# Chunk attention and a SoLU layer: scratch of the squares in the queries' buffers, z's SyncE transfers issued at the turn, sums of w_in's blocks one tile sooner

## The chip, the cores and the metric

One core of a Trainium2 chip. The metric is the device time of one execution in microseconds (us). Its engines here are PE (TensorE, matmuls; PEld is its weight load), DVE (VectorE), ACT (ScalarE), POOL (GpSimd) and SP (SyncE, which only issues transfers). An engine runs its own instructions in the order of the program.

## The reference, cut to what matters

Attention in chunks of 64 positions, then one feed-forward layer with SoLU and a LayerNorm; everything in fp32.

```python
# q, k, v: 8 batches, 8 heads, 576 positions, 64 wide
q_c, k_c, v_c = chunks of 64 positions
s = (q_c @ k_c.T) / 8
p = exp(s - max(s)); p = p / (sum(p) + 1e-9)
x = (p @ v_c), heads side by side          # 4608 tokens x 512
h = x @ w_in                               # 512 -> 1024
e = exp(h - max(h))
solu = h * e / (sum(e) + 1e-9)
ln = (solu - mean) / sqrt(var + 1e-6) * g_ln
out = ln @ w_out                           # 1024 -> 512
```

## The kernel before, in words

The 4608 tokens are 36 tiles of 128. An fp32 product is made on TensorE out of three: each operand is split into a high part (rounded, "top" in the names of the helpers) and the rest ("bottom"), and high x low, high x high and low x high are summed. ACT makes the tops, DVE or POOL the bottoms. A tile passes through these steps: turn of q and k into qT and kT (DVE), scores (PE), softmax (DVE for the row maximum, ACT for the exp, POOL for the division), a turn of the probabilities by 32x32 blocks into a_b (DVE) with four transfers from SBUF to SBUF that put the blocks where they belong (attn_t), values (PE), which gives x with the model's columns on the partitions, the product with w_in (h), exp and SoLU (z), the square for the variance (ACT), a turn of z by 32x32 blocks into z_b (DVE), sixteen transfers z_b to z_t, the split of z_t into z_h and z_l, and the product with w_out into the bank "po" (ffn_out), in three parts called thirds. ACT scales po by r, the inverse of the spread, into o_sb, and SP stores it. Each engine's order is that of the program: the class Order (line 39) keeps it.

Tiles 0 to 4 follow an order written out by hand (START, line 19). Tiles 5 to 9 are single: the loop at line 1192. From tile 10 on the tiles go in pairs (PAIRS, line 97; pair(), line 1089; 13 calls). A pair makes h of two tiles by seven products where eight were needed before (a scheme like Strassen's: the two tiles are the halves of the rows, two halves of d_model, two halves of d_ff; strassen(), line 942). For it w_in's four blocks B11 to B22 need four sums or differences, t1 to t4, and x needs s1 to s4. These are made once, for w_in, by POOL while the single tiles run: t_room (line 880) takes the buffers, t_sum (870) adds blocks into a raw buffer with whole 128x1024 operations, t_top (889, on ACT) and t_bottom (892, on POOL) split that, and t_quarter (896) does sum and split of a quarter on POOL alone, four operations. Where they stand before: t_room and t_sum(B22, B12) at the start of tile 6; t3's top and bottom and t_sum(None, (), B11) after tile 6's variance; t2's top and bottom in tile 7, before solu_b; the last buffers and four quarters of t1 at the start of tile 8; one quarter of t4 after the product of tile 9, three more in pair(10) under `if opening`. The sums of x for pair i+2 are x_sums (line 1050, POOL), x_halves (1058, ACT and POOL) and x_top, x_bottom.

In pair(i) PE runs, in order: a11, s2, s1, s3; three thirds of out1 (tile i-3); s4, a12, a22; the attention of tiles i+2 and i+3 (their values, and scores two tiles on); three thirds of out0 (tile i-2). z_h and z_l of out1 are made at the pair's head, those of out0 beside s4 (z_top, on ACT) and after a22 in program order (z_bottom, on DVE). z_h, z_l and z_b have one buffer, z_t two.

What the change touches:

- variance(i) (line 600) squares z of tiles 0 to 9, spread(i) (line 1033) that of the pairs: ACT writes the squares into a scratch tile "sq", of which only the row sum is used. Both take it from the tag "o_sb" (two buffers), which the scaled output takes too. The queries' tag "qT" (qk_tiles, line 246) has two buffers as well; in pair(i) the order of what spread and turn take is spread(i-1), turn(i+4), turn(i+5), spread(i).
- moves() (line 1070) lists the 16 transfers of z, those with x+y odd on POOL's queue and the others on SP's; pair_moves (1078) returns the list and issue(todo, n) (1084) issues the next n of it. pair(i) makes the list for z of pair i-2 at its head, issues 4 of it after s1 (two on SP, two on POOL), and 12 after attn_turn has turned the probabilities and issued the four moves of attn_t (SP two, and POOL two up to tile 12, later ACT). The two turns of z (pair_turn) are DVE's last work of the pair before.
- The sums of w_in's blocks, as above.

SP also issues the loads of q and k (load_some, up to 9 at two places of a pair), of v, and the stores of the output (store_rest); the loads of a batch are there only in some pairs.

Of the kernel before, what the change touches and what calls it, by code (L numbers as in the profile page):

```python
# [58 lines left out]
def chunk_attention_then_solu_ffn(  # L59
# [13 lines left out]
    DM, FF = H * D, g_ln.shape[0]  # L73
    P = 128
# [784 lines left out]
    TW = {}  # L859
# [10 lines left out]
    def t_sum(of, less, more=()):  # L870

        f = raw_t[0]
        if of is not None:
            pool.tensor_tensor(out=f, in0=f32(of)[0], in1=f32(of)[1], op=ALU.add)
        for x in f32(less):
            pool.tensor_tensor(out=f, in0=f, in1=x, op=ALU.subtract)
        for x in f32(more):
            pool.tensor_tensor(out=f, in0=f, in1=x, op=ALU.add)

    def t_room():  # L880
        def room(dt):
            return work.tile([P, NCH2, HALF], dt, name="t_w", tag="w_a", bufs=5)
        raw_t.append(room(F32))
        TW["t3"] = room(F32R), t_low
        TW["t2"] = room(F32R), room(F32R)
        t1 = room(F32R)
        return lambda: TW.update(t1=(t1, room(F32R)), t4=block(upper, right))
# [145 lines left out]
    def spread(i):  # L1033
        z, esum = st.pop((i, "z"))
        eps = small.tile([P, 1], F32, name="eps")
        act.activation(eps, esum, AF.Square, scale=1e-3, bias=tiny)
        sq = work.tile([P, FF], mybir.dt.bfloat16, name="sq", tag="o_sb")
        ssq = small.tile([P, 1], F32, name="ssq")
        act.activation(sq, z, AF.Square, scale=1.0 / (FF * 32), accum_out=ssq)
        st[i, "v"] = z, ssq, eps  # L1040
# [26 lines left out]
                scores(m + 2)  # L1067
            values(m)

    def moves(zt, of):  # L1070
        for x in range(4):
            for y in range(4):
                yield (pool if (x + y) % 2 else sync).dma_start, (
                    zt[x * 32:(x + 1) * 32, y, of].rearrange("p s a t -> p (s a t)"),
                    turned["b"][y * 32:(y + 1) * 32, x, of].rearrange("p s a t -> p (s a t)"),
                )

    def pair_moves(m, alone=False):
        zt = work.tile([P, 4, 2, NFC, 32], F32, name="z_t")
        for n in (m,) if alone else (m, m + 1):  # L1080
            st[n, "zr"] = zt
        return list(moves(zt, slice(0, 1 if alone else 2)))

    def issue(todo, n):
        for f, args in todo[:n]:
            f(*args)
        del todo[:n]

    def pair(i):
        opening, closing = i == first_pair, i + 2 >= NT  # L1090
        if not banks:
            whole_h.close()
            ps_b = ctx.enter_context(tc.tile_pool(name="ps_b", bufs=1, space=PSUM))
            banks.extend(ps_b.tile([P, HALF], F32, name=n) for n in ("pa", "pb"))
        a, b = banks
        h0, h1 = (work.tile([P, FF], F32, name="z") for _ in range(2))
        HZ[i], HZ[i + 1] = h0, h1
        out1 = queue[0][0]
        softs = pending[:]
        pending.clear()  # L1100
        zmoves = [] if opening else pair_moves(i - 2)

        z_top(out1)
        strassen(i, "a11", a, B11)
        act.copy(h0[:, left], a)
        z_bottom(out1)
        for m in softs[:1]:
            softmax_e(m)
        strassen(i, "s2", b, TW["t2"])
        h_sum(h0[:, right], h0[:, left], b)  # L1110
        x_top(i, "s3")
        x_bottom(i, "s3")
        for m in softs[1:]:
            softmax_e(m)
        strassen(i, "s1", a, TW["t1"])
        issue(zmoves, 4)
        for m in softs:
            whole(softmax_b(m))
        evict()
        strassen(i, "s3", b, TW["t3"])  # L1120
        if not opening:
            spread(i - 1)
        for n in ("s4", "a12", "a22"):
            x_top(i, n)
        h_sum(h1[:, left], h0[:, right], b)
        x_bottom(i, "s4")
        for m in softs:
            attn_turn(m)
        if opening:
            for x in range(1, 4):  # L1130
                t_quarter("t4", B21, TW["t2"], x)
        issue(zmoves, 12)
        least1 = h_out((h1[:, left], h1[:, right]), a, None)
        dve.tensor_tensor(out=h0[:, right], in0=h0[:, right], in1=a, op=ALU.add)
        for p in range(1 if closing else 3):
            product()
        for n in ("a12", "a22"):
            x_bottom(i, n)
        if not opening:
            power(i - 2)  # L1140
            power(i - 1)
        for m in (i + 4, i + 5):
            if m < NT:
                turn(m)
        load_some(9)
        store_rest()

        out0 = queue[0][0]
        waits = (soon.pop(i + 2, []) + soon.pop(i + 3, []))[::-1]
        strassen(i, "s4", a, B22, waits, 6 * NCH2)  # L1150
        if not closing:
            kept.append(out1)
            evict()
            z_top(out0)
        least0 = h_out((h0[:, right], h0[:, right]), a, None)
        strassen(i, "a12", b, B21, waits, 3 * NCH2)
        least0 = h_out((h0[:, left], h0[:, left]), b, least0)
        strassen(i, "a22", a, TW["t4"], waits)
        pair_exp(i, 0, least0)
        least1 = h_out((h1[:, left], h1[:, left]), a, least1)  # L1160
        pair_exp(i, 1, least1)
        if closing:
            return
        z_bottom(out0)
        attention(i)
        for m in (i + 4, i + 5):
            if m < NT:
                load_v(m)
        x_pair(i + 2)
        x_sums(i + 2)  # L1170
        pair_mul(i)
        pair_mul(i + 1)
        for _ in range(3):
            product()
        kept.append(out0)
        pair_mean(i)
        spread(i)
        x_halves(i + 2)
        if i + 4 < NT:
            softmax_a(i + 4)  # L1180
            pending.append(i + 4)
        pair_mean(i + 1)
        pair_turn(i)
        if i + 5 < NT:
            softmax_a(i + 5)
            pending.append(i + 5)
        pair_turn(i + 1)
        load_some(9)
        store_rest()

    first_pair = PAIRS
    for i in range(first, first_pair):
        order.on = i >= ORD
        odd = i % 2 == 1
        turning = i + 1 == first_pair
        if i == first:
            z_turn(i - 1)
            load_batch(next_batch)
            next_batch += 1
        load_v(i + 3)  # L1200
        z_split(queue[0][0], slice(0, NFC))
        if not odd:
            softmax_e(i + 3)
            whole(softmax_b(i + 3))
            attn_turn(i + 3)
            x_high(i + 1)
            if i == first_pair - 4:
                rest_of_room = t_room()
                t_sum(B22, B12)
            if i == first_pair - 2:  # L1210
                rest_of_room()
                for x in range(4):
                    t_quarter("t1", B12, B11, x)
        load_some(LOADS[i][0])
        whole(ffn_in(i))
        if odd:
            for m in (i + 1, i + 2):
                scores(m + 2)
                values(m)
        if turning:  # L1220
            load_v(i + 4)
            for x in range(1):
                t_quarter("t4", B21, TW["t2"], x)
        whole(solu_a(i))
        third()
        if odd:
            softmax_a(i + 3)
            softmax_e(i + 3)
            if turning:
                x_pair(i + 1)  # L1230
                x_sums(i + 1)
            else:
                x_high(i + 1)
        else:
            x_low(i + 1)
        if i == first_pair - 3:
            t_top("t2")
            t_bottom("t2")
        whole(solu_b(i))
        if odd:  # L1240
            if turning:
                x_halves(i + 1)
            else:
                x_low(i + 1)
            whole(softmax_b(i + 3))
            attn_turn(i + 3)
        else:
            for m in (i + 4, i + 5):
                turn(m)
        third()  # L1250
        variance(i)
        if i == first_pair - 4:
            t_top("t3")
            t_bottom("t3")
            t_sum(None, (), B11)
        third()
        load_some(LOADS[i][1])
        z_turn(i)
        store_rest()
        if odd:  # L1260
            softmax_a(i + 4)
            if turning:
                pending.append(i + 4)
# [55 lines left out]
```

## Time and profile before

| | |
|---|---|
| Two timed runs | 527.69 and 529.74 us, median 528.72 |
| The profiled execution's own time | 529.91 us |
| Its span, first to last instruction | 528.1 us |
| Mean granted TensorE clock | 0.976 |
| Busy: PE | 473.2 us, 90% of the span, 4115 matmuls |
| PEld | 364.2 us, 69% |
| DVE | 362.4 us, 69% |
| POOL | 315.9 us, 60% |
| ACT | 285.4 us, 54% |
| Moved by DMA | 72.06 MB, mean 136 GB/s |

The page's slices cut the span into 40 parts of 13.2 us; a digit is the busy share in tenths, and 9 is 90% or more:

```profile
PE   6889998999948699888999988999799989898997
ACT  2568853546514282728292738282747383838461
POOL 0358475398999665656665745647474747475540
PEclk9999999899988799999999999989999999998999
```

How to read rows of a timeline: start in us, length in us (of a run of equal instructions, of all of them), engine, operation, tiles written <- tiles read, shape, count, and in brackets the idle time ahead of it and what ended it. In a row of busy times by stage each engine's busy us stand with its count of instructions, then the granted clock (1.00 is full), the DMA engines' mean busy share and GB/s. All instructions are recorded at line 50, where a helper issues them, so rows are told apart by their tiles.

### The profile page before, as it was taken

Reading aid. Unit: us, or ns where it says so; the run is one execution under the profiler, and the core shown is the slowest. Engines: PE = TensorE matmul, PEld = TensorE weight load, DVE = VectorE, ACT = ScalarE, POOL = GpSimd, SP = SyncE. Lnnn points to the kernel's source line nnn. Section 1 sums busy time; section 2 is a strip of 40 time slices with the busy share of each in tenths; the row PEclk is TensorE's granted clock in tenths of the full one; section 3 lists DMA queues with packets and bytes.
Section 4 is the critical chain, followed back from the end, with each engine's and each line's share of the span. In section 5 each row is a group of like instructions: output and inputs, shape, how many; then the busy total and the mean of one; then the engine's idle time right before and its main releaser. Section 6 shows DMA issues by size and latency. Waiting matters only on the chain.

```text
span 528.1 us, 11438 instructions
## 1 busy us (share of the span) xinstructions
PE 473.2 (90%) x4115; PEld 364.2 (69%) x4115; DVE 362.4 (69%) x580; ACT 285.4 (54%) x509; POOL 315.9 (60%) x470
## 2 busy tenths in 40 slices
PE   6889998999948699888999988999799989898997
PEld 5647886877736487666776756767566767676776
DVE  2999974959845286768686758576587777765441
ACT  2568853546514282728292738282747383838461
POOL 0358475398999665656665745647474747475540
PEclk9999999899988799999999999989999999998999
DMA  9999778486843915957525957495743434351331
GB/s 244 303 213 303 138 131 216 107 177 118 193 98 92 164 27 124 177 120 157 147 60 129 173 120 155 112 152 144 139 126 96 114 88 119 83 132 38 91 99 40
DMA packets 193768, 72.06 MB, mean 136 GB/s; under 512 B 177129, under 2 KB 177649, under 8 KB 193329
## 3 DMA queue, kind: packets, MB, share of 16 engines
q1 hardware_dynamic: 186528, 58.63, 50.3%
q0 software_dynamic: 4736, 9.45, 7.2%
q10 hardware_dynamic: 2448, 3.28, 2.4%
q8 instruction: 32, 0.52, 0.4%
q14 instruction: 24, 0.19, 0.1%
HBM read 36.70 MB, written 9.44 MB: 87 GB/s over the span
## 4 chain that ended last, share of the span: by engine, by line
PE 38%; SPq 18%; POOL 12%; ACT 9%; DMA 9%; DVE 7%; issue 6%; ACTq 0%; DVEq 0%; POOLq 0%
PE po L50 22%; SPq L50 18%; PE pa L50 6%; PE ph L50 5%; PE pb L50 4%; POOL t_f L50 4%; POOL t_w L50 3%; DVE z_l L50 3%; ACT z_h L50 3%; DMA out_dram<-o_sb 3%; ACT z L50 3%; DMA z_t<-z_b 3%; DVE a_b L50 2%; POOL e L50 1%; DMA nat<-in_k_dram 1%
## 5 line engine op out<-in xcount | busy, mean ns | idle before, releaser
L50 PE MATMUL po<-wo_l,z_h 128*128 128x512 f32 x280 | 112.9, 403 | 8.0 <-ACT z_h L50 7.9
L50 PE MATMUL po<-wo_h,z_l 128*128 128x512 f32 x280 | 113.0, 404 | 7.4 <-DVE z_l L50 7.4
L50 PE MATMUL po<-wo_h,z_h 128*128 128x512 f32 x280 | 111.4, 398 | 0.0
L50 POOL TENSOR_TENSOR x_s<-x_p 128x256 f32<-128x256 f32 x26 | 26.2, 1010 | 88.2 <-ACT x_p L50 87.2
L50 POOL DMA_DIRECT2D z_t<-z_b x136 | 68.7, 511 | 12.1 <-DVE z_b L50 10.3
L50 DVE TENSOR_TENSOR z_l<-z_t,z_h 128x1024 fp32r<-128x1024 f32 (+1 forms) x36 | 41.3, 1146 | 48.0 <-ACT z_h L50 37.8
L50 PEld LDWEIGHTS po<-wo_h,z_l 128*128 128x128 f32 x280 | 53.7, 192 | 24.8 <-DVE z_l L50 13.8
L50 ACT CAST z_h<-z_t 128x1024 fp32r<-128x1024 f32 (+1 forms) x36 | 34.8, 967 | 63.3 <-DMA z_t<-z_b 56.6
L50 PEld LDWEIGHTS po<-wo_l,z_h 128*128 128x128 f32 x280 | 53.8, 192 | 20.6 <-ACT z_h L50 9.8
L50 POOL TENSOR_TENSOR x_t<-x_p,x_t 128x256 fp32r<-128x256 f32 x65 | 47.7, 745 | 29.2 <-ACT x_t L50 24.8
L50 PEld LDWEIGHTS po<-wo_h,z_h 128*128 128x128 f32 x280 | 53.7, 192 | 10.9
L50 ACT ACTIVATE o_sb<-po,r 128x512 f32<-128x512 f32 (+1 forms) x36 | 24.4, 677 | 65.5 <-DMA attn_t<-a_b 38.7
L50 PE MATMUL pa<-wi_h,x_t 128*128 128x512 f32 x156 | 50.9, 407 | 8.3 <-POOL x_t L50 7.1
L50 DVE STREAM_TRANSPOSE z_b<-z 128x1024 f32<-128x1024 f32 x33 | 40.8, 1236 | 24.0 <-ACT z L50 20.9
L50 ACT ACTIVATE sq<-z 128x1024 bf16<-128x1024 f32 x36 | 37.7, 1048 | 18.9 <-DMA out_dram<-o_sb 18.9
L50 PEld LDWEIGHTS pa<-wi_h,x_t 128*128 128x128 f32 x156 | 30.0, 193 | 17.9 <-POOL x_t L50 7.5
L50 ACT ACTIVATE z<-z,z_sum 128x1024 f32<-128x1024 f32 x34 | 39.1, 1149 | 3.2 <-DVE z L50 3.1
L50 PE MATMUL pb<-t_w,x_t 128*128 128x512 f32 x130 | 37.8, 405 | 3.2 <-ACT x_t L50 1.9
L50 POOL TENSOR_TENSOR e<-e,s_rinv 128x512 f32<-128x512 f32 x31 | 32.3, 1061 | 9.3 <-DVE s_rinv L50 9.0
L50 ACT ACTIVATE z_b<-z,h_nmax 128x1024 f32<-128x1024 f32 x26 | 29.7, 1143 | 15.0 <-DVE h_nmax L50 14.9
L50 ACT CAST x_t<-x_p 128x256 fp32r<-128x256 f32 x65 | 25.1, 403 | 17.4 <-POOL x_p L50 14.2
L50 PE MATMUL pa<-wi_l,x_t 128*128 128x512 f32 x78 | 31.5, 404 | 1.5 <-DVE z L50 1.2
(136 smaller groups left out, 1003.5 us busy)
## 6 DMA issues: line engine op xcount, KB each, us to landing
out_dram<-o_sb SPq DMA_DIRECT2D x35, 256.0 KB, 2.8
z_t<-z_b SPq DMA_DIRECT2D x128, 64.0 KB, 2.1
z_t<-z_b POOLq DMA_DIRECT2D x128, 64.0 KB, 2.6
q_st<-in_q_dram SPq DMA_DIRECT2D x96, 72.0 KB, 3.3
k_st<-in_k_dram SPq DMA_DIRECT2D x96, 72.0 KB, 2.8
v_sb<-in_v_dram SPq DMA_DIRECT2D x27, 256.0 KB, 4.5
w_raw<-in_moe_w_out_dram SPq DMA_DIRECT2D x4, 1024.0 KB, 7.5
attn_t<-a_b SPq DMA_DIRECT2D x60, 64.0 KB, 3.5
```

The lines of the kernel that those rows point to most:

```text
L50: ins = make(*args, **kwargs)
```

## The change

Three parts. First, spread()'s scratch takes its buffer from the tag qT in place of o_sb; variance() keeps o_sb. Second, moves() is split by queue: pair_moves issues SP's eight transfers at once, at the head of pair(i) (and of the last tile but one), and returns POOL's eight, of which two are issued after s1 and the other six where twelve were issued before. Third, the sums of w_in's blocks move: t_room and t_sum(B22, B12) after tile 5's variance; t3's top and bottom and the sum with B11 at the start of tile 6; t2's top and bottom after tile 6's variance, together with the last buffers and quarters 0 and 1 of t1; quarters 2 and 3 stay at the start of tile 8; all four quarters of t4 stand in pair(10).

```diff
@@ -1034,7 +1034,7 @@
         z, esum = st.pop((i, "z"))
         eps = small.tile([P, 1], F32, name="eps")
         act.activation(eps, esum, AF.Square, scale=1e-3, bias=tiny)
-        sq = work.tile([P, FF], mybir.dt.bfloat16, name="sq", tag="o_sb")
+        sq = work.tile([P, FF], mybir.dt.bfloat16, name="sq", tag="qT")
         ssq = small.tile([P, 1], F32, name="ssq")
         act.activation(sq, z, AF.Square, scale=1.0 / (FF * 32), accum_out=ssq)
         st[i, "v"] = z, ssq, eps
@@ -1067,19 +1067,22 @@
                 scores(m + 2)
             values(m)
 
-    def moves(zt, of):
+    def moves(zt, of, odd):
         for x in range(4):
             for y in range(4):
-                yield (pool if (x + y) % 2 else sync).dma_start, (
-                    zt[x * 32:(x + 1) * 32, y, of].rearrange("p s a t -> p (s a t)"),
-                    turned["b"][y * 32:(y + 1) * 32, x, of].rearrange("p s a t -> p (s a t)"),
-                )
+                if (x + y) % 2 == odd:
+                    yield (pool if odd else sync).dma_start, (
+                        zt[x * 32:(x + 1) * 32, y, of].rearrange("p s a t -> p (s a t)"),
+                        turned["b"][y * 32:(y + 1) * 32, x, of].rearrange("p s a t -> p (s a t)"),
+                    )
 
     def pair_moves(m, alone=False):
         zt = work.tile([P, 4, 2, NFC, 32], F32, name="z_t")
         for n in (m,) if alone else (m, m + 1):
             st[n, "zr"] = zt
-        return list(moves(zt, slice(0, 1 if alone else 2)))
+        of = slice(0, 1 if alone else 2)
+        issue(list(moves(zt, of, 0)), 8)
+        return list(moves(zt, of, 1))
 
     def issue(todo, n):
         for f, args in todo[:n]:
@@ -1113,7 +1116,7 @@
         for m in softs[1:]:
             softmax_e(m)
         strassen(i, "s1", a, TW["t1"])
-        issue(zmoves, 4)
+        issue(zmoves, 2)
         for m in softs:
             whole(softmax_b(m))
         evict()
@@ -1127,7 +1130,7 @@
         for m in softs:
             attn_turn(m)
         if opening:
-            for x in range(1, 4):
+            for x in range(4):
                 t_quarter("t4", B21, TW["t2"], x)
         issue(zmoves, 12)
         least1 = h_out((h1[:, left], h1[:, right]), a, None)
@@ -1205,11 +1208,12 @@
             attn_turn(i + 3)
             x_high(i + 1)
             if i == first_pair - 4:
-                rest_of_room = t_room()
-                t_sum(B22, B12)
+                t_top("t3")
+            if i == first_pair - 4:
+                t_bottom("t3")
+                t_sum(None, (), B11)
             if i == first_pair - 2:
-                rest_of_room()
-                for x in range(4):
+                for x in range(2, 4):
                     t_quarter("t1", B12, B11, x)
         load_some(LOADS[i][0])
         whole(ffn_in(i))
@@ -1219,8 +1223,6 @@
                 values(m)
         if turning:
             load_v(i + 4)
-            for x in range(1):
-                t_quarter("t4", B21, TW["t2"], x)
         whole(solu_a(i))
         third()
         if odd:
@@ -1233,9 +1235,6 @@
                 x_high(i + 1)
         else:
             x_low(i + 1)
-        if i == first_pair - 3:
-            t_top("t2")
-            t_bottom("t2")
         whole(solu_b(i))
         if odd:
             if turning:
@@ -1249,10 +1248,15 @@
                 turn(m)
         third()
         variance(i)
+        if i == first_pair - 5:
+            rest_of_room = t_room()
+            t_sum(B22, B12)
         if i == first_pair - 4:
-            t_top("t3")
-            t_bottom("t3")
-            t_sum(None, (), B11)
+            t_top("t2")
+            t_bottom("t2")
+            rest_of_room()
+            for x in range(2):
+                t_quarter("t1", B12, B11, x)
         third()
         load_some(LOADS[i][1])
         z_turn(i)
```

## Rows read from the trace of the kernel before

**Rows 1.** Busy by stage: span, PE, PEld, DVE, ACT, POOL, PEclk, DMA share, GB/s.

```profile
186.17:209.41 23.24, 23.23 (x226) 18.67 (x218) 17.66 (x33) 12.81 (x25) 15.93 (x25) 1.00 0.33 76
209.41:476.76 267.35, 243.04 (x2120) 184.02 (x2116) 192.81 (x331) 149.49 (x281) 160.18 (x250) 0.99 0.57 127
288.81:316.82 28.01, 24.60 (x218) 18.24 (x218) 19.34 (x34) 15.01 (x29) 16.04 (x25) 1.00 0.71 144
```

**Rows 2.** Chain of waits in order of time: start, us, what.

```profile
417.71 1.26 SPq L50
421.74 2.05 DMA z_t<-z_b
424.26 1.05 ACT z_h L50
```

**Rows 3.** Timeline of SP's queue and of POOL, one cycle.

```profile
409.13 1.21 SPq L50 DMA_DIRECT2D z_t<-z_b  x2
...
414.83 2.82 SPq L50 DMA_DIRECT2D attn_t<-a_b  x4
...
417.71 4.62 SPq L50 DMA_DIRECT2D z_t<-z_b  x6
...
414.67 2.99 POOL L50 DMA_DIRECT2D z_t<-z_b  x6
```

**Rows 4.** Timeline of PE; in brackets the idle time before and what ended it.

```profile
425.36 0.50 PE L50 MATMUL po<-wo_l,z_h 128*128 128x512 f32 x1 [0.41 <-ACT z_h L50]
...
426.62 0.50 PE L50 MATMUL po<-wo_h,z_l 128*128 128x512 f32 x1 [0.53 <-DVE z_l L50]
...
435.07 1.66 PE L50 MATMUL pa<-t_w,x_t 128*128 128x512 f32 x6 [0.42 <-ACT z L50]
```

**Rows 5.** Square's tile: total wait (us), times; below, ACT's timeline.

```profile
  DMA out_dram<-o_sb: 18.9, 9
...
302.99 0.69 ACT L50 ACTIVATE o_sb<-po,r 128x512 f32<-128x512 f32 x1 [3.02 <-DMA out_dram<-o_sb]
```

**Rows 6.** Timeline of POOL, tiles 5 to 10.

```profile
100.28 4.02 POOL L50 DMA_DIRECT2D z_t<-z_b  x8 [1.10 <-DVE z_b L50]
...
107.25 2.42 POOL L50 TENSOR_TENSOR t_w<-wi_h,wi_l 128x1024 f32<-128x1024 f32 x1
...
151.80 0.71 POOL L50 TENSOR_TENSOR t_f<-wi_h,wi_l 128x256 f32<-128x256 f32 x1
...
155.34 0.72 POOL L50 TENSOR_TENSOR x_s<-x_p 128x256 f32<-128x256 f32 x1
...
178.92 1.41 POOL L50 TENSOR_TENSOR x_t<-x_p,x_t 128x256 fp32r<-128x256 f32 x2
```

**Rows 7.** Timeline of ACT, tiles 6 to 9.

```profile
114.67 1.05 ACT L50 CAST t_w<-t_w 128x1024 fp32r<-128x1024 f32 x1 [3.89 <-POOL t_w L50]
...
116.21 1.03 ACT L50 CAST z_h<-z_t 128x1024 fp32r<-128x1024 f32 x1
...
145.08 0.57 ACT L50 COPY x_p<-sy 128x512 f32<-128x512 f32 x1
```

**Rows 8.** Timeline of PE, tiles 7 to 10.

```profile
119.32 0.50 PE L50 MATMUL po<-wo_h,z_l 128*128 128x512 f32 x1 [1.15 <-DVE z_l L50]
...
136.22 0.47 PE L50 MATMUL ph<-wi_l,x_h 128*128 128x512 f32 x1 [0.71 <-DVE z L50]
...
179.70 1.22 PE L50 MATMUL pb<-wi_h,x_t 128*128 128x512 f32 x2 [4.90 <-POOL x_t L50]
```

**Rows 9.** Timeline of DVE and POOL, a stretch in which both ran.

```profile
117.28 1.99 DVE L50 TENSOR_TENSOR z_l<-z_t,z_h 128x1024 fp32r<-128x1024 f32 x1 [5.37 <-ACT z_h L50]
...
118.27 3.25 POOL L50 TENSOR_TENSOR t_w<-t_w,wi_h 128x1024 f32<-128x1024 f32 x1
```

**Rows 10.** DMA issues: moves of attn_t by SP, times, KB, median us to landing.

```profile
attn_t<-a_b SPq DMA_DIRECT2D x60, 64.0 KB, 3.5
```


## The prediction, made before the change had run

> **What bounds the kernel now.** I read the slices of the page first: PE is busy nearly everywhere, so the question is where it waits, and the slices show two places, a hole near 140 to 180 us and a small loss in every pair after 186. Then the busy time by stage [rows 1]. A pair of tiles asks the same PE work each time. From the first product of one pair's out0 to that of the next, the first such cycle takes 23.24 us with PE busy for 23.23 of them; the ten that follow take 267.35, a mean of 26.74, with PE busy 24.30 of each. So 3.50 us per cycle, 35.0 in all, is not PE work. The first cycle is the one in which the transfers of z were long done (z_turn(9) had made them), which makes it a sample of a pair without that wait.
>
> The chain of waits [rows 2] says what the others wait for: SP issues z's moves, the last of them lands, ACT makes z_h, DVE z_l, then the products. The queues show why it is late [rows 3]: SP issues two moves when z is turned (409.13), stands until a_b is turned, issues the four attn_t moves (414.83), and only from 417.71 to 422.33 the other six of z. POOL's last six are out by 417.66, 4.7 us sooner. PE's own timeline [rows 4] shows the bill: 0.41 for z_h, 0.53 for z_l, and 0.42 for ACT's copy of the first product, late because ACT did z_h late. Each such stop also costs a slower first product. A second cause is on ACT: squares and output copies share two buffers, and wait for output stores [rows 5]: 18.9 us before nine squares, 3.02 before one copy.
>
> The hole at 140 to 180 is POOL's: the eight quarters of t1 and t4 stand in its queue before the x sums [rows 6].
>
> **The change part by part.**
>
> *z's moves on SP.* Same sixteen issues per pair; SP's eight now stand at the head of the pair, wait only for the second turn of z (ending at 409.1), and are out after some 5.8 us (1.21 for two and 4.62 for six [rows 3]), before a_b is turned: attn_t is not pushed back. POOL issues two and then six at the same places as before. The last transfer is then POOL's at 417.66, landing some 2.1 to 2.6 later, near 420.3, against 424.26 when z_h began. z_h fits while PE is in s4, a12 and a22; ACT is idle there. DVE's z_l still stands behind the last row maximum, and that ends while PE is in the attention. So both PE waits go, and ACT's work after them moves up by 2 to 3 us, so the copy of the first product is no longer late. Next in line are the attn_t moves (landing 3.5 us after issue [rows 10]) and, with loads in the queue, SP itself.
>
> *Squares in the queries' buffers.* Only spread()'s squares move, those of the pairs. qT of both tiles is read by the scores before spread(i), and spread(i-1) ends before the next turn, so no wait comes in; the 18.9 and 3.02 us [rows 5] go. They mostly delay ACT and DVE, and through them a PE product in some pairs.
>
> The two together: a cycle is bounded by 23.24 below and 26.74 above [rows 1]. I take 23.4 for the five cycles without much loading, as they come closest to the sample, and 24.6 for the five in which q and k are loaded (such a one takes 28.01 now with the DMA engines 0.71 busy): a mean of 24.0, so 10 x 2.74 = 27.4 us. The closing pair loses its z_l stop too: 0.8. Cover: if POOL's late half bound z_h instead, half of this would go.
>
> The Trainium skill speaks against much of a gain here: by "DMA: Bandwidth & Descriptors" (Issuing engines are not separate DMA queues), transfers of all issuers run on the same sixteen engines, and who issues saves only the issue time, usually small. By that rule the gain is only what the issue was held back, and this trace shows that 8.6 us passed between SP's second and third move of z; no run here shows the moves issued otherwise.
>
> *Sums one tile sooner.* The squares of tiles 0 to 9 are variance()'s, which keeps its buffers; only POOL's and ACT's queues change here. POOL was free at 99.2 (100.28 less the 1.10 it idled) [rows 6]. t_sum takes three operations of 2.42, so it runs from 99.2 to 106.6 instead of from 107.25. The z moves (4.02) and attn_t moves (half of that) stand behind it now, until 112.6. Then t_bottom (2.4) and two sums with B11 (4.9): 119.9. t_top("t3") has its sum at 106.6, shortly before ACT has to start the exp of that tile. t_top("t2") now stands on ACT before z_h of tile 4, which ran at 116.21 [rows 7], and waits for 119.9: copy 1.05, output copy and z_h 1.7, z_l 1.2, so the first product with z_l comes at 123.9 instead of 119.32 [rows 8], 4.6 us later. That is the price of the move, and PE carries it to the next tiles.
>
> What it buys stands at the other end. PE waited 0.71 for DVE before ffn_in(9) [rows 8], so between 3.9 and 4.6 of the delay arrives there; I take 4.2. The copy of x that POOL's sums for tile 10 need, done at 145.65 [rows 7], comes at 149.9. POOL has only two quarters of t1 in that tile (7.3 of the 14.6), and none of t4: with moves of 4.0 and 2.0 that follow z_b and a_b, both 4 later, it is done near 146. The x sums start at once, at 149.9 instead of 155.34 [rows 6], 5.4 sooner. But from the sums to x_bottom of a12 it is 155.34 to 178.92, 23.6 us of a POOL that hardly rests, and one more quarter of t4 now stands in it (3.54, from 151.80 to 155.34): 27.1. So 177.0 instead of 178.92: the a12 product, which waited 4.90 for it [rows 8], comes 1.9 sooner.
>
> Bounds of the opening: 5.4 us early, if the fourth quarter hides in POOL's short rests and the delay at tile 4 is partly absorbed; 3.7 late, if the long POOL operations are stretched by DVE (below, C). I take 1.9 early, from the rows.
>
> **Sum.** The profiled run: span 528.1, whole 529.91, which is 1.2 above the median of 528.72. 529.9 - 1.9 - 27.4 - 0.8 = 499.8; put against the median, 498.6, so 498.5.
>
> **Rivals.**
> A. *The wait passes to attn_t.* Those moves land 3.5 us after their issue [rows 10], about when a22 starts, and PE already waits there by tenths. If a_b does not move up when PE does, what is won before a12 is waited for behind it, and a cycle falls only to about 25.5: 529.9 - 1.9 - 12.4 - 1.2 = 514.5. For it: the small waits now. Against: a_b stands behind DVE's sum of s3, so it moves with PE; and the sample cycle had the same moves.
> B. *SP's head start changes nothing*, because z_h is held by something else (POOL's half, the z_h buffer): 529.9 - 1.9 - 1.2 = 527. For it: eight of sixteen moves stay where they were. Against: these were out 4.7 us before SP's, and ACT stood idle before z_h.
> C. *Slower: the sums on ACT and POOL in the opening.* Place: t_top("t2") before z_h of tile 4, and four quarters of t4 instead of three in pair(10). Point: x sums later than 151.8 (178.92 less 27.1) are paid in full. Price: z_l took 1.99 and the POOL sum beside it 3.25 [rows 9], against the 2.42 of [rows 6]. With 0.8 more on each of five long POOL operations and 1.6 for DVE behind them, the sums start at 155.5, 3.7 late. The kernel is slower by it if the pairs give less than that, so if z was hidden anyway: 529.9 + 3.7 - 1.2 = 532.5.
>
> The Trainium skill states for C, in "SBUF — State Buffer" (Who interferes with whom), that a VectorE operation with two inputs in SBUF and a GpSimd one that reads SBUF shut each other out. The trace agrees with its pair of 1.99 and 3.25.
> D. *The shared buffer holds DVE in the pairs*: the turn of the next queries now waits for the square before it. If ACT is as late there as it was behind the stores (3.02), the turn and the row maximum behind it lose up to 1 us a cycle: 529.9 - 1.9 - 17.4 - 1.2 = 509.5. Against: that lateness is what the change takes away.
>
> **How the numbers follow.** Forecast 0.60 (its own range 490 to 508), A 0.18, D 0.06, B 0.11, C 0.05. About 2% can be told from no change: 518.1 and 539.3. Forecast and D are faster, A too for most of its spread; B and C lie within 2%, but for a part of C with PE at its lower clock after the longer wait: faster 0.80, same 0.18, slower 0.02. The range: below, cycles of 23.24 and an opening 5.4 early give 487; above, A with half of it gone again is near 519. I give 488 to 519.
>
> **What would show it.** Right: SP issues eight z moves in one row at the turn; z_h of out0 starts some 3 us before the attention ends; cycles near 24; no square of a pair waits for an output store; PE waits some 5 us before the first product of tile 4; x sums near 150, PE's a12 near 178. Wrong: waits for attn_t that grow to 2 us a cycle (A), z_h no sooner (B), x sums near 155 (C), turns of q that wait for ACT (D).

## The result, and the profile after

The changed kernel took 503.67 us (median of two runs, 503.45 and 503.90), against 528.72: a ratio of 0.9526, 95% interval 0.9445 to 0.9608. Four more runs on another chip gave 502.76 us against 529.16, a ratio of 0.9487 (0.9462 to 0.9511). The forecast was 498.5 us with a range of 488 to 519: the direction and the size held, 5 us were not gained.

The profiled execution took 503.45 us. From its page: the span, then busy tenths in 40 slices, here of 12.54 us.

```profile
span 501.7 us, 11452 instructions
PE   6799999877899839999999999999999999999997
PEclk9899999998799959999999999999999999999999
```

The small loss in every pair is gone from PE's row: every slice from 188 us on but the last has its 9. The hole did not go. It used to lie near 140 to 180 us; now there is a shallow one near 100 to 138 and a deep one in the slice at 176, with the clock down in both.

The busy time by stage, in the columns of [rows 1]: the ten pair cycles, then the most heavily loaded of them.

```profile
213.51:451.09 237.58, 235.02 (x2123) 184.48 (x2117) 197.75 (x331) 149.34 (x279) 165.02 (x250) 1.00 0.63 141
285.43:309.38 23.95, 23.66 (x224) 18.46 (x218) 20.11 (x34) 15.13 (x30) 16.46 (x25) 1.00 0.77 161
```

A mean of 23.76 in place of 26.74, and 23.95 where 28.01 stood, though the DMA engines are busier (0.77 for 0.71). PE's own busy time fell too, from 24.30 to 23.50 a cycle. Part of that is the stops that are gone: in [rows 4] the products behind a stop take 0.50, where most of their kind take 0.39. How much of the 0.8 it is was not measured. So of the 29.8 us won in the ten cycles 21.8 are waiting and 8.0 are PE's busy time. Whatever PE still waited for in these ten cycles is this (waits; us in total, times, longest):

```profile
PE pa L50 <- DMA attn_t<-a_b: 1.8, 6, 0.4
PE pa L50 <- ACT z L50: 0.3, 2, 0.2
```

Neither z_h nor z_l is in the list. One cycle on SP, POOL and ACT, to be held against [rows 2, 3]:

```profile
389.74 5.58 SPq L50 DMA_DIRECT2D z_t<-z_b  x8
395.44 2.81 SPq L50 DMA_DIRECT2D attn_t<-a_b  x4
...
395.27 2.98 POOL L50 DMA_DIRECT2D z_t<-z_b  x6
...
401.75 1.05 ACT L50 CAST z_h<-z_t 128x1024 fp32r<-128x1024 f32 x1 [2.39 <-DMA attn_t<-a_b]
...
405.32 0.50 PE L50 MATMUL po<-wo_l,z_h 128*128 128x512 f32 x1
```

SP's eight moves stand in one row and are out 0.12 us before attn_t's. POOL's six are the last to leave, at 398.25. z_h starts 12.0 us after SP's first move; in [rows 2, 3] it was 15.1. It ends 2.5 us before PE needs it at 405.32. What holds z_h now is POOL's half of the moves: POOL's last, issued at 397.76, landed 3.8 us later, 0.2 us before z_h started, and that distance is the same in all ten cycles. (The bracket names attn_t, which z_h does not read.)

Now the opening, where the forecast failed. POOL from tile 5 on, to be held against [rows 6]:

```profile
100.90 2.40 POOL L50 TENSOR_TENSOR t_w<-wi_h,wi_l 128x1024 f32<-128x1024 f32 x1
103.38 3.26 POOL L50 TENSOR_TENSOR t_w<-t_w,wi_h 128x1024 f32<-128x1024 f32 x1
106.72 2.74 POOL L50 TENSOR_TENSOR t_w<-t_w,wi_l 128x1024 f32<-128x1024 f32 x1
109.40 4.00 POOL L50 DMA_DIRECT2D z_t<-z_b  x8
113.39 1.96 POOL L50 DMA_DIRECT2D attn_t<-a_b  x4
...
155.40 0.73 POOL L50 TENSOR_TENSOR x_s<-x_p 128x256 f32<-128x256 f32 x1 [3.32 <-ACT x_p L50]
...
183.15 1.40 POOL L50 TENSOR_TENSOR x_t<-x_p,x_t 128x256 fp32r<-128x256 f32 x2
```

ACT's copies of t3 and t2, and the z_h behind the second, to be held against [rows 7]:

```profile
109.49 1.05 ACT L50 CAST t_w<-t_w 128x1024 fp32r<-128x1024 f32 x1 [5.30 <-POOL t_w L50]
...
122.73 1.05 ACT L50 CAST t_w<-t_w 128x1024 fp32r<-128x1024 f32 x1 [7.41 <-POOL t_w L50]
...
124.26 1.03 ACT L50 CAST z_h<-z_t 128x1024 fp32r<-128x1024 f32 x1
```

And PE's stops in the same stretch, to be held against [rows 8]:

```profile
113.05 0.77 PE L50 MATMUL ph<-wi_l,x_h 128*128 128x512 f32 x1 [2.83 <-DVE z L50]
...
118.43 0.50 PE L50 MATMUL ph<-wi_h,x_h 128*128 128x512 f32 x1 [0.82 <-DMA attn_t<-a_b]
...
125.34 0.50 PE L50 MATMUL po<-wo_l,z_h 128*128 128x512 f32 x1 [2.01 <-ACT z_h L50]
...
127.34 0.80 PE L50 MATMUL po<-wo_h,z_l 128*128 128x512 f32 x1 [1.26 <-DVE z_l L50]
...
183.93 1.22 PE L50 MATMUL pb<-wi_h,x_t 128*128 128x512 f32 x2 [8.53 <-POOL x_t L50]
```

Four stops of 6.9 us in all where [rows 8] has one of 1.15 and one of 0.71. The first has two parts. ACT's exp waited for t3's copy (109.49 above), and DVE's division of the probabilities (POOL's in most tiles) came late: it ran beside POOL's second sum and took 1.93 in place of 0.69. The row before, then the row after:

```profile
103.30 0.69 DVE L50 TENSOR_TENSOR e<-e,s_rinv 128x512 f32<-128x512 f32 x1
```

```profile
105.26 1.93 DVE L50 TENSOR_TENSOR e<-e,s_rinv 128x512 f32<-128x512 f32 x1
```

By the time x of tile 10 is copied the kernel is 9.7 us later than before, POOL has run out of work and stands idle for 3.32 us, and then the longer chain of four quarters makes the first a12 wait 8.53 in place of 4.90.

Against that stands a stop that [rows 8] does not have and that is gone. In the kernel before, the first product of tile 10's pair waited 7.08 us for POOL; in the changed kernel it does not wait:

```profile
157.60 1.22 PE L50 MATMUL pa<-wi_h,x_t 128*128 128x512 f32 x2 [7.08 <-POOL x_t L50]
```

The stretch from tile 5's product to the first product of out0 in pair(10), in the columns of [rows 1], before and after:

```profile
81.97:186.17 104.20, 86.43 (x819) 68.19 (x818) 64.79 (x95) 44.03 (x73) 77.88 (x110) 0.92 0.69 143
```

```profile
83.90:189.67 105.77, 86.44 (x820) 68.34 (x818) 66.88 (x94) 44.01 (x73) 79.38 (x109) 0.90 0.69 141
```

PE is busy for the same time in both, so the 1.6 us more are waiting: some 5.1 more in the stops above, 3.6 more at a12, and 7.1 less before the pair.

### The profile page after: what moved, and what is told of

Its sections match the earlier page's. It is cut to its first block, busy times and chain, and to the rows that moved or that the text cites. A ratio compares the mean times of both kernels' runs of the same rounds, so it can differ in the third digit from the quotient of the medians.

```text
span 501.7 us, 11452 instructions
## 1 busy us (share of the span) xinstructions
PE 465.7 (93%) x4115; PEld 364.9 (73%) x4115; DVE 371.9 (74%) x580; ACT 287.5 (57%) x509; POOL 322.8 (64%) x470
## 2 busy tenths in 40 slices
DMA packets 193767, 72.06 MB, mean 144 GB/s; under 512 B 177128, under 2 KB 177648, under 8 KB 193328
## 4 chain that ended last, share of the span: by engine, by line
PE 49%; DMA 15%; SPq 10%; DVE 9%; POOL 7%; ACT 5%; issue 4%; ACTq 0%; DVEq 0%; POOLq 0%
PE po L50 23%; SPq L50 10%; DMA attn_t<-a_b 9%; PE pa L50 9%; PE ph L50 8%; PE pb L50 3%; PE sx L50 3%; PE sy L50 3%; DMA nat_z<-in_q_dram 2%; DMA z_t<-z_b 2%; POOL t_f L50 2%; DVE a_b L50 2%; DVE z_b L50 1%; DVE w_a L50 1%; ACT z_h L50 1%
## 5 line engine op out<-in xcount | busy, mean ns | idle before, releaser
L50 PE MATMUL po<-wo_h,z_l 128*128 128x512 f32 x280 | 111.1, 397 | 2.1 <-DVE z_l L50 2.1
L50 POOL TENSOR_TENSOR x_s<-x_p 128x256 f32<-128x256 f32 x26 | 23.5, 906 | 65.2 <-ACT x_p L50 64.2
L50 ACT ACTIVATE z_b<-z,h_nmax 128x1024 f32<-128x1024 f32 x26 | 29.8, 1148 | 21.5 <-DVE h_nmax L50 21.1
L50 PEld LDWEIGHTS pa<-wi_h,x_t 128*128 128x128 f32 x156 | 29.8, 191 | 11.0 <-DMA attn_t<-a_b 5.0
L50 PE MATMUL pb<-t_w,x_t 128*128 128x512 f32 x130 | 36.2, 391 | 1.3 <-POOL x_t L50 1.3
L50 DVE SCALAR_TENSOR_TENSOR z<-z,z_b 128x1024 f32<-128x1024 f32 x26 | 36.2, 1425 | 0.0
```

Of the source, the lines that this page charges most:

```text
L50: ins = make(*args, **kwargs)
```

## The experiments

Times below are medians of four runs, or of ten for the sums alone, against the kernel before on the same chip (527.92, 527.06 and 529.16 us in the three groups). The ratios, each with its 95% interval in parentheses, are what can be compared across the groups. "Opening" is the time from tile 5's product (at 81.97 us before, 83.90 after) to the first product of out0 in pair(10); it leaves out the start of the program, which the change does not touch and which alone differed by up to 1.9 us between profiles. The opening was 104.20 before and 105.77 after; "ten cycles" were 267.35 and 237.58. One profile has some scatter: in the four runs below whose sums stand where they stood before, the opening was 104.26, 104.61, 104.19 and 103.05.

**The parts taken alone.** First, the squares and the moves, with the sums left where they were: the diff without its hunks on t_room, t_top, t_bottom, t_sum and t_quarter.

> The change without its third part: squares in qT's buffers and SP's eight moves of z at the head, the sums of w_in's blocks where they were. Theory (the third part costs 3.5 to 4.1 us, the tenth pair's a12 waits for one more quarter of t4): 500 us, 3.5 to 4 below the whole change, and PE's wait before the first a12 is near 4.9 again in place of 8.5. Rival (the later opening is not the sums' doing, or they pay for themselves elsewhere): 503 to 505 us.

501.31 us, a ratio of 0.9491 (0.9464 to 0.9518). Ten cycles 237.73, opening 104.26, a12 waits 4.91. In the profile the sums cost 1.5 us of opening (0.5 against the second profile of the whole change further down). That is within the scatter of the opening, it is not the 3.5 to 4.1 that I expected, and the times do not separate this kernel from the whole change, whose second ratio was 0.9487.

The squares alone:

```diff
-        sq = work.tile([P, FF], mybir.dt.bfloat16, name="sq", tag="o_sb")
+        sq = work.tile([P, FF], mybir.dt.bfloat16, name="sq", tag="qT")
```

> The first part alone: only the squares' scratch moves to qT's buffers. Theory (the stops for z_h and z_l carry the gain, the squares' waits for stores mostly lay beside them): 523 to 526 us; the 18.9 us of waits before squares fall under 7, PE's waits for z_h and z_l stay near 15 us in all. Rival 1 (the squares' waits were the cause of the late copies, and these of the rest): 510 us or less. Rival 2 (neither part gives anything without the other): 528 us or more.

520.69 us, a ratio of 0.986 (0.9832 to 0.9888): faster than expected, and neither rival. Ten cycles 257.25. The square's tile, then what PE waited for in these cycles:

```profile
  DMA out_dram<-o_sb: 6.2, 1
```

```profile
PE po L50 <- DVE z_l L50: 5.3, 10, 0.5
PE po L50 <- ACT z_h L50: 5.2, 8, 1.6
PE pa L50 <- ACT z L50: 4.3, 10, 0.4
PE pb L50 <- DMA attn_t<-a_b: 0.2, 1, 0.2
```

The wait that is left before a square is one of 6.2 at tile 4, a square of variance(). The three stops of [rows 4] are still there in most of the ten cycles.

SP's moves alone: the hunks on moves(), pair_moves() and issue(zmoves, 2).

> The second part alone: only SP's eight moves of z go to the head of the pair. Theory (the late SP moves are the main cause): 504 to 508 us; PE's waits for z_h and z_l fall from 15 us to about 5; the squares still wait some 19 us for stores, which costs PE a few tenths in some pairs. Rival 1 (squares the cause, z's head start hidden): 523 us or more. Rival 2 (neither without the other): 520 us or more.

501.54 us, a ratio of 0.9499 (0.9468 to 0.953); ten cycles 237.84. The square's tile, and PE's waits in these cycles:

```profile
  DMA out_dram<-o_sb: 7.8, 6
```

```profile
PE pa L50 <- DMA attn_t<-a_b: 2.5, 8, 0.5
```

The moves alone give all that both give. The squares, untouched here, wait 7.8 us instead of 18.9: less than I expected, and no product waits behind it. So the squares' 7 us and the moves' 26 us are not a sum. I read it so that the squares' waits cost PE something only as long as ACT was late for z; no run shows that step by itself.

The sums alone: only the hunks that the first run left out.

> The third part alone: only the sums of w_in's blocks move. Theory (they cost the opening 3.5 to 4 us and nothing pays that back later): 532 to 533 us, the ten pair cycles as long as before (267 us). Rival (the sums begin sooner and give 2 us, as I had predicted, where the rest of the change is not there): 526 to 527 us.

528.20 us, a ratio of 1.0012 (0.9983 to 1.004): neither the 4 us that I expected nor the 2 that I had predicted. The opening is 104.29 against 104.20, with the same stops as in the whole change (2.84, 1.72 and 1.27, a12 8.52). The ten cycles, which this edit does not touch, were 263.92, so these differ by some 3 us between profiles of the old pairs.

**How many moves must be ahead.** The squares and the moves, with four of SP's eight at the head:

```diff
-        issue(list(moves(zt, of, 0)), 8)
-        return list(moves(zt, of, 1))
+        mine = list(moves(zt, of, 0))
+        issue(mine, 4)
+        return list(moves(zt, of, 1)) + mine
```

> The first two parts, but only four of SP's eight moves of z at the head of the pair, and the other four behind the moves of attn_t. Theory (z_h waits for the last of z's transfers, so what counts is when the last leaves SP): between the ends, 505 to 512 us, with PE's waits for z_h and z_l back in part. Rival 1 (fewer moves behind attn_t are hidden, all that counted was that SP was cleared): 501 to 502 us. Rival 2 (any move behind attn_t costs the whole): 519 to 521 us.

506.27 us, a ratio of 0.9586 (0.9544 to 0.9629); ten cycles 243.94, a third of the way from 237.73 back to the 257.25 of the squares alone. SP and ACT in one cycle:

```profile
391.10 2.48 SPq L50 DMA_DIRECT2D z_t<-z_b  x4
396.81 2.85 SPq L50 DMA_DIRECT2D attn_t<-a_b  x4
399.75 3.08 SPq L50 DMA_DIRECT2D z_t<-z_b  x4
```

```profile
404.72 1.05 ACT L50 CAST z_h<-z_t 128x1024 fp32r<-128x1024 f32 x1 [4.01 <-DMA z_t<-z_b]
```

z_h starts 13.6 us after the first move, between 12.0 and 15.1. Over the ten cycles of the three kernels with the squares moved, with two, four and eight of SP's moves ahead of attn_t's, the means are 14.4, 13.0 and 12.1. The time follows the last move out of SP, and neither rival holds. PE's stops for z_h and z_l came back in one cycle only (0.8 and 0.5); the rest of the loss is in stops for ACT's copy and attn_t and in slower products.

**Where the opening goes.** The whole change, with one quarter of t4 put back in tile 9:

```diff
             load_v(i + 4)
+            for x in range(1):
+                t_quarter("t4", B21, TW["t2"], x)
...
-            for x in range(4):
+            for x in range(1, 4):
                 t_quarter("t4", B21, TW["t2"], x)
```

> The whole change, but the first quarter of t4 stands again in tile 9, after the loads of v. Theory (POOL stood idle 3.3 us ahead of the sums of x, the quarter of 3.7 fits there, and the first a12 waits one quarter less): x sums within 0.5 us of where they were against tile 9, PE's wait before a12 near 5 in place of 8.5, 500 to 501 us. Rival (the quarter only pushes the sums of x and a12 as far as before): 503 to 504 us.

498.43 us, a ratio of 0.9447 (0.9401 to 0.9493); opening 101.91. POOL's sums of x and PE's a12:

```profile
155.28 0.73 POOL L50 TENSOR_TENSOR x_s<-x_p 128x256 f32<-128x256 f32 x1
```

```profile
179.65 1.22 PE L50 MATMUL pb<-wi_h,x_t 128*128 128x512 f32 x2 [4.58 <-POOL x_t L50]
```

The sums of x begin where they did, with no idle time before them: the quarter lies in the hole. The opening is 3.9 us shorter than in the whole change (2.8 against its second profile), about the 3.54 of the quarter that the prediction had counted. It is also shorter than in each of the four runs whose sums were not moved, 2.3 shorter than in the first two parts alone: with this quarter left in the hole, the other moved sums gain in the opening. The intervals of the ratios overlap, so both gains rest on the profiles.

Next, whether t3's copy ahead of the exp is what makes x late: the whole change, with t3's top, bottom and the sum with B11 behind tile 6's exp.

```diff
-            if i == first_pair - 4:
-                t_top("t3")
-            if i == first_pair - 4:
-                t_bottom("t3")
-                t_sum(None, (), B11)
...
         whole(solu_a(i))
+        if i == first_pair - 4:
+            t_top("t3")
+            t_bottom("t3")
+            t_sum(None, (), B11)
```

> The whole change, but t3's top, its bottom and the sum with B11 stand behind tile 6's exp in place of ahead of it. Theory (my step that failed: t3's top held ACT's exp, PE stood 2.8 us and then ran at the lower clock, so x of tile 10 came late and POOL stood idle 3.3 us before the sums of x): the stop before the product of tile 7 goes, POOL's idle time before the sums of x falls below 1 us, 500 to 501 us. Rival (the lateness comes from t2's top ahead of z_h and from the late moves of attn_t, and t3's place costs nothing): 503 to 504 us, POOL idle 3 us as before.

503.62 us, a ratio of 0.9505 (0.9479 to 0.953), beside 502.76 for the whole change. The theory fell; its rival held. PE's stops in that stretch:

```profile
111.49 0.47 PE L50 MATMUL ph<-wi_l,x_h 128*128 128x512 f32 x1 [1.49 <-DVE z L50]
...
117.47 0.50 PE L50 MATMUL ph<-wi_h,x_h 128*128 128x512 f32 x1 [2.75 <-DMA attn_t<-a_b]
...
125.07 0.50 PE L50 MATMUL po<-wo_l,z_h 128*128 128x512 f32 x1 [2.74 <-ACT z_h L50]
```

What the stop for z lost, and more, those for attn_t and z_h took. So t3's place counts for 1.3 us of the 2.83; in what is left DVE's division still takes 1.93 beside POOL's second sum. POOL is idle 3.29 us before the sums of x, as before. The whole change once more, on the chip of this run:

> The whole change once more, on the chip of the three runs beside it. Both theories: 503 to 505 us, some 2 above the first two parts alone, with PE's wait before the first a12 near 8.5.

502.76 us, by ratio the same as the first two parts alone (0.9487 and 0.9491), so the 2 us above them that both theories expected do not show; a12 waited 8.55 as expected, and the opening was 104.75.

**Another order of the sums.** The first two parts, with the sums laid out anew (the diff shows the new places; the old ones are taken out):

```diff
         z_split(queue[0][0], slice(0, NFC))
+        if i == first_pair - 5:
+            rest_of_room = t_room()
+            t_sum(B22, B12)
+        if i == first_pair - 3:
+            t_top("t2")
+            t_bottom("t2")
+            rest_of_room()
+            for x in range(2):
+                t_quarter("t1", B12, B11, x)
...
             load_v(i + 4)
+            for x in range(1):
+                t_quarter("t4", B21, TW["t2"], x)
...
         variance(i)
+        if i == first_pair - 5:
+            t_top("t3")
```

So t4's first quarter is in tile 9 here too, as in the kernel before.

> The first two parts, with the sums of w_in's blocks laid out anew: B22+B12 at the start of tile 5, where POOL stood idle 7.4 us; t3's top after tile 5's variance, its bottom and the sum with B11 at the start of tile 6; t2's top, bottom and two quarters of t1 in tile 7 right after the split of z; two quarters of t1 in tile 8, one of t4 in tile 9. Theory (POOL alone sets when the sums of x begin and when the first a12 can run, from tile 5 to the tenth): the 7 us idle before the first product of tile 10's pair goes, a12 comes 7 to 9 us sooner, 492 to 494 us. Rival (ACT's tops and the late moves of z and attn_t take it back, as in the change): 499 to 502 us.

495.83 us, a ratio of 0.9383 (0.9333 to 0.9434): short of the expected 492 to 494. Opening 100.38. PE's stop before tile 10's pair is 0.66, where the first two parts alone have 7.04; the wait before a12 is 4.88. A new stop of 2.64 us had come at tile 5. Its cause, on POOL and DVE:

```profile
91.29 2.35 POOL L50 TENSOR_TENSOR t_w<-wi_h,wi_l 128x1024 f32<-128x1024 f32 x1
91.39 3.34 DVE L50 TENSOR_TENSOR z_l<-z_t,z_h 128x1024 fp32r<-128x1024 f32 x1 [3.97 <-ACT z_h L50]
```

The same, with the first sum waiting until this z_l is done:

```diff
-            t_sum(B22, B12)
+            t_sum(B22, B12, behind=z_low)
```

> The kernel with the sums laid out anew, with one more wait: the first sum of w_in's blocks starts only when DVE's z_l of tile 4 is done. Theory (z_l took 3.3 us in place of 1.2 because both operations read two operands from SBUF at once, and PE waited 2.6 for it): z_l takes 1.2 to 1.5 us, no stop at that place, 1.5 to 2.5 us below the run without the wait, 493 to 494.5 us. Rival (the lost time is made up before tile 10, POOL's chain is just as long): the same 495 to 496 us.

```profile
92.93 1.23 DVE L50 TENSOR_TENSOR z_l<-z_t,z_h 128x1024 fp32r<-128x1024 f32 x1 [4.35 <-ACT z_h L50]
...
94.23 2.37 POOL L50 TENSOR_TENSOR t_w<-wi_h,wi_l 128x1024 f32<-128x1024 f32 x1 [1.37 <-DVE z_l L50]
```

z_l took 1.23, the stop was 0.53, the opening 98.91, so 1.5 shorter. The time was 496.72 us, a ratio of 0.9379 (0.9355 to 0.9402): by ratio the same as without the wait, so in the time the rival held, and the profile alone shows a gain. But a collision of the same sort had come up further on: with the sums later, the third of them met one of DVE's divisions, which took 2.77 in place of 0.69.

```profile
99.35 2.77 DVE L50 TENSOR_TENSOR e<-e,s_rinv 128x512 f32<-128x512 f32 x1
```

Last, the bottoms of a12 and a22 ahead of t4's quarters, first without that wait and then with it.

```diff
         if opening:
+            for n in ("a12", "a22"):
+                x_bottom(i, n)
             for x in range(1, 4):
```

> As the kernel with the sums laid out anew, and in the first pair the bottoms of a12 and a22 stand ahead of the three quarters of t4 on POOL. Theory (a12 needs no t4, only a22 does; POOL's work in all is the same): a12 runs under the last quarter, 0.5 to 1.5 us below the run without it. Rival (a22 waits for t4 just as long as a12 did, and the swap gives nothing): the same time within 0.3 us.

> That wait, and the bottoms of a12 and a22 ahead of t4's three quarters. Theory: 0.4 to 0.8 us below the run with the wait alone, as from s3 to the next pair's first product it was 22.5 us without the swap and 21.9 with it. Rival (a22 waits for t4 instead, no gain): within 0.3 us of it.

498.08 us (0.9424, 0.9377 to 0.9471) and 497.44 us (0.9384, 0.9357 to 0.9411). a12 no longer waits, a22 does, for 4.68 us. The openings were 100.39 and 98.40, against 100.38 and 98.91 without the swap. The swap gives not more than 0.5 us, and the times do not show it.

## Why the prediction was right, and where it was not

By terms, on the two profiles (501.7 less 528.1 is -26.4):

| Term | predicted | measured |
|---|---|---|
| start of the program, to tile 5's product | 0 | +1.9 (83.90 for 81.97) |
| opening | -1.9 | +1.6 (105.77 for 104.20) |
| first cycle | 0 | +0.6 (23.84 for 23.24) |
| ten cycles | -27.4 | -29.8 (237.58 for 267.35) |
| closing | -0.8 | -0.7 (50.61 for 51.34) |

So the forecast came close in part by luck: the pairs gave 2.4 us more than predicted, which covered two thirds of the 3.5 us by which the opening was wrong; the 1.9 at the start is a difference between two profiles.

**z's moves on SP: right, and more alone than I said.** The mechanism was read correctly from the chain and the two queues: the last transfer sets z_h, and six on SP stood behind attn_t. Three doses show it (z_h 15.1, 13.6 and 12.0 us after the first move in the cycles shown, with two, four and eight of SP's moves ahead of attn_t's). Predicted 24.0 a cycle, measured 23.76; the heavily loaded cycles came down to 24 like the others. What the rows bounded below, 23.24, was the right end. Two readings in it were off. "3.50 us per cycle ... is not PE work" is the distance to the sample cycle; PE's idle time was 2.43 a cycle, and the other 1.07 was PE busy for longer than in the sample. And POOL's last transfer was to land "2.1 to 2.6 later": it took 3.8, so POOL's half does bind z_h now, the case against which the prediction covered itself. It costs PE nothing here, since z_h is ready 2.5 us before PE needs it. z_h starts 3.6 us before the attention ends, where "some 3" was said. The Trainium skill's "DMA: Bandwidth & Descriptors" (Issuing engines are not separate DMA queues) says that transfers from all issuers run on the same engines, and that issuing from several of them at once saves only the time to issue, usually a small one. The trace does not contradict it, but that sentence is not what decided here: the moves and their bytes are the same (72.06 MB on both pages), each is issued by the same engine as before, and what was won is the time for which six of SP's moves stood behind attn_t's. The prediction put that at 8.6 us between SP's second and third move; by [rows 3] 7.4 us passed between them, and 8.6 from the start of the first.

**Squares: right that no wait comes in, wrong to lump them.** "The two together" hid that the second part suffices (501.54 against 501.31). Rival D did not occur: no turn of q waited for a square, and with the squares or without them the ten cycles were 237.7 and 237.8.

**A and B fell.** attn_t is next in line, as A said, but for 1.8 us in ten cycles and not for 2 in each. B would have left the cycles at 26.7.

**The opening: the failed step.** It was "t_top("t2") now stands on ACT before z_h [...] That is the price of the move". The first product with z_l was to come 4.6 us later; it came at 127.34, 8.0 later, of which the start of the program is 1.9, and PE's wait there was 2.01 and 1.26 us in place of "some 5". I wrote that the moves of z and attn_t stand behind the sums "until 112.6" and charged nothing for it; I wrote that t3's sum ends "shortly before" the exp and left it there. In the changed kernel the three sums took 8.6 us, not 7.3, DVE's division beside them 1.93, not 0.69, POOL had the attn_t moves out at 115.35, t3's top held ACT's exp, and x of tile 10 was 9.7 us late, of which the start of the program is 1.9. So POOL's sums of x began at 155.40 in place of 149.9, with POOL idle, and "one more quarter of t4 now stands in it" was then paid in full, as in C. PE's a12 came at 183.93, not near 178. What the prediction had no term for on the other side is the 7.08 us stop before tile 10's pair, which the change took away. Putting the quarter back won 2.8 to 3.9 us of opening. Which of the earlier stops counts is not settled by one edit: when t3's top is moved, the stop passes to attn_t and z_h. That they come from the three sums standing ahead of the moves fits the run in which the sums stand elsewhere (opening 98.91), but that run changed more than this, and the cause stays open.

**C was right about its place and part of its price, and wrong that it could decide.** The collision of DVE and POOL that it counted came true beside the moved sums, 0.8 and 0.3 us more on two of POOL's operations and 1.2 on DVE's division. With the moves giving 26 us, an opening at most 1.6 us longer cannot turn the sign.

## What to carry to other kernels

When a set of transfers is split over queues, look for the last one to leave any queue and at what stands before it there: the order within one queue was worth 26 us of 528 here, without one byte less moved. When work is moved earlier on an in-order engine, charge every transfer and every release that now stands behind it, and then look whether the engine runs dry later: an operation that filled a hole should stay in the hole. And two gains found in one profile need not add: try each alone.

## What the runs showed of the hardware that I had not expected

DVE's z_l, started 0.10 us after a POOL operation that also reads two operands from SBUF, took 3.34 us in place of 1.23 and ended 1.09 us after POOL's: it ended as if it had begun only when POOL was done. DVE's division did the same twice, with 1.93 and 2.77 us in place of 0.69; both times it ended 0.55 us after POOL's sum. [Rows 9] looked like a mutual slowing, 1.99 and 3.25, but with the POOL row ahead of them they fit the same rule:

```profile
115.80 2.39 POOL L50 TENSOR_TENSOR t_low<-t_w 128x1024 fp32r<-128x1024 f32 x1 [0.37 <-ACT t_w L50]
```

z_l ended 1.08 us after that operation, and the sum that started beside z_l ended 2.25 us after z_l. The Trainium skill's "SBUF — State Buffer" (Who interferes with whom) states such an exclusive hold; the trace agrees, with 3.34.

After two stops PE ran for a while at the lower of its two clocks (1.2 GHz), for which the prediction's sum has no term of its own. After the stops of 2.01 and 1.26 us the granted clock of the stage was 0.65:

```profile
125.34:135.12 9.78, 8.51 (x25) 6.50 (x26) 9.64 (x12) 4.68 (x8) 9.02 (x13) 0.65 0.82 126
```

The kernel before has a stop for the same z_l of 1.15 us there, kept a granted clock of 1.00 and took 7.00 for that stage, so some 2.7 of the 9.78 us are slower products. Over the whole opening this does not add up to a loss, PE being busy for 86.43 us before and 86.44 after: in the kernel before, the slow products stand behind the 7.08 us stop (two in 1.22 at 157.60).
